# Moving g's high parts, the weights, x and g's low parts to other residues modulo 512 bytes in SBUF

## The chip, the cores and the metric

The kernel runs on one core of a Trainium2 chip. The metric is the time of one execution in microseconds (us) of device time. Before the change three runs gave a median of 848.11 us.

## The reference

Eight batches of eight heads (sequence 576, head dimension 64) go through a linear attention: q is normalised over the head dimension, k over the sequence, and q meets the 64x64 product of k and v. The result, seen as 4608 rows of 512, goes through a two-layer network with relu squared between the layers.

```
q_s = exp(q - max(q, axis=-1));  q_s = q_s / (sum(q_s, axis=-1) + 1e-09)
k_s = exp(k - max(k, axis=2));   k_s = k_s / (sum(k_s, axis=2) + 1e-09)
kv  = einsum('bhsd,bhse->bhde', k_s, v)
x   = einsum('bhsd,bhde->bhse', q_s, kv)  -> (4608, 512)
r   = maximum(x @ w_in, 0)                # (4608, 2048)
g   = s * (r * r) + b
out = g @ w_out                           # (4608, 512), all float32
```

## The kernel before

The precision of float32 is reached with three matmuls where one would do. Each operand is split into a high part of type float32r, which TensorE takes in one pass, and a low part (the remainder, float32r too). A product is high by high, high by low and low by high. So x is held as xh and xl, each weight as w[:, 0] and w[:, 1], and g as gh and gl.

The 4608 rows are taken in blocks of 512 tokens, the last block being the 64 left-over rows of all eight batches. For each block and each of 16 chunks of 128 of the 2048 hidden columns there is one step t. It has two halves:

- `h_parts` (L1328): 12 matmuls of 512 columns make h for the chunk. The stationary operand is a 128x128 piece of a weight tile `w`, the moving operand is a 512-wide row of xh or xl.
- `o_parts` (L1400): 12 matmuls of 512 columns add the chunk to four accumulators. The stationary operand is a 128x128 piece of gh or gl, the moving operand is a 512-wide row of a weight tile `w`. For each quarter j the order is (gh, w high), (gh, w low), (gl, w high).

Between them ScalarE takes relu out of PSUM into `r` (L1353), ScalarE and VectorE square, scale and shift it, ScalarE rounds it into gh, and VectorE writes gl = r - gh (L1363, L1372, L1379 and others). `gh` and `gl` have two buffers each in the pool `gpool`, used in turn, and `r` has one. Four of the blocks go through a scheme with seven products in place of eight (`product`, L1123; "q" and "qa" in the rows). The last block's second layer is `final` (L1314; "last" in the rows). Its gh and gl lie in weight tiles, not in `gpool`.

Attention of later batches runs beside this on the other engines, a few of its matmuls (L352 kv, L489, L499, L791) between the steps. Every matmul has its load of the stationary operand, an instruction of its own (LDWEIGHTS, engine PEld in the rows), which runs while the matmul before it is still under way.

The order of all instructions on an engine is fixed by hand: generators yield pieces, `Order.run` plays them against planned times, and the list `FIRST` fixes the first ones. `tc.manual_schedule` keeps that order. The tile pools then decide only the addresses, each pool's tiles one after the other in the order of the pools, and the waits that follow from the buffers. Nearly all of SBUF is in use.

Addresses below are bytes within a partition. Most large tiles are a multiple of 512 bytes long, so one shift at the head moves all of them alike. Before the change a tile of 128 bytes with no use but its size (`tiny.tile([P, 32], F32, name="before", ...)`) stands in the first pool, and all the large tiles start at 0 modulo 512. Slices of 128 columns are 512 bytes and rows of 512 columns 2048 bytes, so every stationary piece and every moving row of the 512-column matmuls starts at 0 modulo 512 too.

Of the kernel before, what the change touches and what calls it, by code (L numbers as in the profile page):

```python
# [8 lines left out]
F32 = mybir.dt.float32  # L9
F32R = mybir.dt.float32r  # L10
# [15 lines left out]
def attention_moe(ctx: ExitStack, tc: tile.TileContext, q, k, v, w_in, w_out, s, b, out):  # L26
# [51 lines left out]
    def pool(name, bufs=1):  # L78
        return ctx.enter_context(tc.tile_pool(name=name, bufs=bufs))

    tiny, const, work = pool("tiny", 4), pool("const"), pool("work")
    gpool, xpool, wpool = pool("gpool", 2), pool("xpool", 2), pool("wpool", NFC + 1)
    wide_, small, ends, qpool, sums_q = pool("wide"), pool("small", 4), pool("ends"), pool("qpool", 2), pool("sums", 2)
    dram = ctx.enter_context(tc.tile_pool(name="dram", bufs=1, space=bass.MemoryType.DRAM))
    ps = ctx.enter_context(tc.tile_pool(name="ps", bufs=1, space=bass.MemoryType.PSUM))


    tiny.tile([P, 32], F32, name="before", tag="before", bufs=1)
    ident = const.tile([P, P], F32, name="ident")
    make_identity(nc, ident)  # L90

    kvboth = const.tile([P, 2, 2, 2, D], F32, name="kvf")
    kvfs = [kvboth[:, i] for i in range(2)]
    nc.gpsimd.memset(kvboth, 0.0)
    sb = ends.tile([P, 24], F32, name="sb")
    s_col, b_col = sb[:, 0:1], sb[:, 1:2]
    half = [slice(h * D, (h + 1) * D) for h in range(2)]

# [280 lines left out]
    def k_stream(u):  # L379
        pr, i = divmod(u, 2)  # L380
        due, (tag, bufs) = DUE_K[u], wide(u)
        yield Op("PE", 1.1, due, needs=[f"k{u} there"], take=["big", "ke"])
        kt = by_head(tiles[pr][0])[:, 2 * i:2 * i + 2]
        kT = ps.tile([P, 2, 512], F32, name=f"kT_{u}", tag="big").rearrange("p a b -> p (a b)")
        for n in range(NT):
            for h in range(2):
                nc.tensor.matmul(kT[half[h], n * P:(n + 1) * P], kt[:, h, n], ident, start=True, stop=True)
        yield Op("DVE", 0.67, due)
        km = tiny.tile([P, 1], F32, name=f"km_{u}", tag="km")
        nc.vector.tensor_reduce(out=km, in_=kT[:, 0:S], axis=AX.X, op=ALU.max, negate=True)  # L390
        yield Op("ACT", 0.78, due, free=["big"], gives=[f"z{u}"])
        if pr not in zs:
            zs[pr] = tiny.tile([P, 2], F32, name=f"z_{pr}", tag="z")
        ke = early[:, 0:S]
        nc.scalar.activation(ke, kT[:, 0:S], AF.Exp, bias=km, accum_out=zs[pr][:, i:i + 1])

        yield Op("PE", 0.55, due, take=[tag], free=["ke"])
        kn = ps.tile([P, 2, 512], F32, name=f"kn_{u}", tag=tag, bufs=bufs).rearrange("p a b -> p (a b)")
        for n in range(NQ):
            nc.tensor.transpose(kn[:, n * P:(n + 1) * P], ke[:, n * P:(n + 1) * P], ident)  # L400
        nc.tensor.transpose(kn[0:LEFT, TB:TB + P], ke[:, TB:S], ident)
        yield Op(KN_ON[u], 0.7 if KN_ON[u] == "ACT" else 0.82, due, free=[tag], gives=[f"k{u}"])
        copy = copier(KN_ON[u])
        copy(kt[:, :, 0:NQ], kn[:, 0:TB].rearrange("p (n h d) -> p h n d", n=NQ, h=2))
        copy(kt[0:LEFT, :, NQ], kn[0:LEFT, TB:TB + P].rearrange("p (h d) -> p h d", h=2))
# [29 lines left out]
    def kv_second(pr):  # L435
        due = DUE_V[pr]
        yield Op("PE", 1.4, due, needs=[f"k{u}" for u in (2 * pr, 2 * pr + 1)] + [f"v{pr} there"], take=["sm"], gives=[f"kv{pr}"])
        kv = ps.tile([P, 512], F32, name=f"kv_{pr}", tag="sm", bufs=1)[:, 0:2 * (D + 1)].rearrange("p (u e) -> p u e", u=2)
        heads(kv, by_head(tiles[pr][0]).rearrange("p (u h) n d -> p u h n d", u=2), v_of(tiles[pr][2]))
        yield Op("DVE", 0.33, due)  # L440
        z = tiny.tile([P, 2], F32, name=f"z_{pr}", tag="z")
        scales(z, kv[:, :, D])
        yield Op("ACT", 1.03, due, free=["sm"], gives=[f"kvf{pr}"])
        blocks(pr, kv[:, :, 0:D], z)
# [14 lines left out]
    def q_stream(u):  # L459
        pr, i = divmod(u, 2)  # L460
        bb, hp = divmod(u, NP)
        due, (tag, bufs) = DUE_Q[u], wide(u)

        before = [f"kv{NP // 2 - 1}"] + [f"qe{u}" for u in range(NP - 2, NP)]
        yield Op("DVE", 0.76, due, needs=[f"q{pr} {i} there" if pr == 0 else f"q{pr} there"])
        qt = by_head(tiles[pr][1])[:, 2 * i:2 * i + 2]
        qm = small.tile([P, 2, NT], F32, name=f"qm_{u}", tag="qm")
        nc.vector.tensor_reduce(out=qm, in_=qt, axis=AX.X, op=ALU.max)
        yield Op("DVE", 0.73, due)
        nc.vector.tensor_tensor(out=qt, in0=qt, in1=bc(qm, [P, 2, NT, D]), op=ALU.subtract)  # L470
        yield Op("ACT", 0.74, due, take=["qe"], gives=[f"qe{u}"])
        qn = qpool.tile([P, 2 * NT * (D + 1)], F32, name=f"qe_{u}", tag="qe", bufs=2)
        qe = qn.rearrange("p (n h e) -> p n h e", h=2, e=D + 1)

        nc.gpsimd.memset(qe[:, :, :, D:D + 1], 1e-9)
        nc.scalar.activation(qe[:, :, :, 0:D].rearrange("p n h d -> p h n d"), qt, AF.Exp)
        yield Op("DVE", 0.74, due)
        qs = sums_q.tile([P, NT, 2], F32, name=f"qs_{u}", tag="qs", bufs=2)
        nc.vector.tensor_reduce(out=qs, in_=qe, axis=AX.X, op=ALU.add)
        yield Op("DVE", 0.18, due)  # L480
        nc.vector.reciprocal(qs, qs)
        yield Op("DVE", 0.73, due)

        qn = qn[:, 0:NT * P].rearrange("p (n h d) -> p n h d", h=2, d=D)
        nc.vector.tensor_tensor(out=qn, in0=qe[:, :, :, 0:D], in1=bc(qs, [P, NT, 2, D]), op=ALU.mult)
        yield Op("PE", 0.6, due, take=[tag, "qf"], free=["qe"])
        qT = ps.tile([P, 2, 512], F32, name=f"qT_{u}", tag=tag, bufs=bufs).rearrange("p a b -> p (a b)")
        for n in range(NT):
            nc.tensor.transpose(qT[:, n * P:(n + 1) * P], qn[:, n].rearrange("p h d -> p (h d)"), ident)  # L489
        yield Op(QF_ON[u], 0.55 if QF_ON[u] == "ACT" else 0.66, due, free=[tag])  # L490
        qf = early[:, NT * P:NT * P + S]
        copier(QF_ON[u])(qf, qT[:, 0:S])
        yield Op("PE", 1.0, due, needs=[f"kvf{pr}"] + before * (bb > 0), take=[tag], free=["qf"])

        HB = TB // 2
        xh, xl = x_tile(bb)
        xp = ps.tile([P, 2, 512], F32, name=f"xp_{u}", tag=tag, bufs=bufs)
        for a, src in enumerate((slice(0, HB), slice(HB, S))):
            nc.tensor.matmul(  # L499
                xp[:, a, 0:src.stop - src.start], kvfs[pr % 2][:, i].rearrange("p h d -> p (h d)"), qf[:, src],  # L500
                start=True, stop=True
            )
        yield Op("ACT", 0.82, due, needs=[f"out{u - 4}"] if u >= 4 else (), gives=[f"left{u} there"])
        xh, xl = [t[:, hp, :].rearrange("p (a c) -> p a c", a=2) for t in (xh, xl)]
        nc.scalar.copy(xh, xp[:, :, 0:HB])
        nc.scalar.copy(left_of(u), xp[:, 1, HB:HB + LEFT])
        yield Op("DVE", 0.6, due, free=[tag], gives=[f"x{u}"])
        nc.vector.tensor_tensor(out=xl, in0=xp[:, :, 0:HB], in1=xh.bitcast(F32), op=ALU.subtract)


    def k_tiles(pr):
        m2 = bits[:, 2 * P:6 * P].rearrange("p (h n d) -> p h n d", h=4, n=2)
        m1 = bits[:, 6 * P:8 * P].rearrange("p (h d) -> p h d", h=4)
        return m2, m1, tiny.tile([P, 2], F32, name=f"km_{pr}", tag="km")

    def k_max_2(kt, m2):
        nc.vector.tensor_tensor(out=m2, in0=kt[:, :, 0:2], in1=kt[:, :, 2:4], op=ALU.max)
# [106 lines left out]
    def q_late(u):  # L624
# [9 lines left out]
        if on_act:  # L634
            yield Op("ACT", 0.6, due, take=["qe"])
            qe = qpool.tile([P, 2, 2, NT, SQ], F32, name=f"qe_{u}", tag="qe", bufs=2)
            qs = sums_q.tile([P, 2, NT], F32, name=f"qs_{u}", tag="qs", bufs=2)
            for h in range(2):
                for n in range(NT):
                    if (h, n) in ((0, 2), (0, 4), (1, 1), (1, 3)):  # L640
# [6 lines left out]
        else:  # L647
# [4 lines left out]
            qe = qpool.tile([P, 2, 2, NT, SQ], F32, name=f"qe_{u}", tag="qe", bufs=2)  # L652
            nc.scalar.activation(qe, qt_, AF.Exp)
            yield Op("DVE", 0.76, due)
            qs = sums_q.tile([P, 2, 2, NT], F32, name=f"qs_{u}", tag="qs", bufs=2)
            nc.vector.tensor_reduce(out=qs, in_=qe, axis=AX.X, op=ALU.add)
            yield Op("DVE", 0.5, due)
            nc.vector.scalar_tensor_tensor(
# [50 lines left out]
    def kv_late(pr):  # L709
# [10 lines left out]
        kv = kv[:, 0:2 * (D + 1)].rearrange("p (u e) -> p u e", u=2)  # L720
        heads(kv, by_head(kt).rearrange("p (u h) n d -> p u h n d", u=2), v_of(vt))
        yield Op("DVE", 0.5, due)
        z = tiny.tile([P, 2], F32, name=f"z_{pr}", tag="z")
        nc.vector.tensor_scalar(z, kv[:, :, D], 1e-9, None, op0=ALU.add)
        nc.vector.reciprocal(z, z)

# [465 lines left out]
    def quadrant(p, n):  # L1192
# [59 lines left out]
            w = win(t % NFC)  # L1252
            gh, gl = w[:, 0], w[:, 1]
        else:
            gh = gpool.tile([P, TB], F32R, name=f"gh_{t}", tag="gh")
            gl = gpool.tile([P, TB], F32R, name=f"gl_{t}", tag="gl")
        G[t] = (gh, gl)
        if on:
# [10 lines left out]
    def second_block(n):  # L1269
# [12 lines left out]
        yield Op("ACT", 0.52, due, needs=[there], take=["g"])  # L1282
        if n < 2:
            r = kept(f % 2)
        gh = gpool.tile([P, TB], F32R, name=f"gh_{t}", tag="gh")
        gl = gpool.tile([P, TB], F32R, name=f"gl_{t}", tag="gl")
        G[t] = (gh, gl)
        nc.scalar.copy(gh, r)
# [28 lines left out]
    G = {}  # L1317
    acc = {}

    def h_parts(t):  # L1320

        blk, f = divmod(t, NFC)
# [9 lines left out]

    def g_tiles(t):
        r = gpool.tile([P, TB], F32, name=f"r_{t}", tag="r", bufs=1)
        gh = gpool.tile([P, TB], F32R, name=f"gh_{t}", tag="gh")
        gl = gpool.tile([P, TB], F32R, name=f"gl_{t}", tag="gl")
        G[t] = (gh, gl)
        return r, gh, gl
# [257 lines left out]
```

## Time and profile before

| | |
|---|---|
| median of 3 runs (lowest, highest) | 848.11 us (848.05, 848.28) |
| the profiled execution's own time | 849.44 us |
| its span, first to last instruction | 847.6 us |
| mean granted TensorE clock in the span | 0.997 of 2.4 GHz |
| TensorE matmul busy | 835.3 us, 99% of the span |
| VectorE, ScalarE, GpSimd busy | 574.5, 517.3, 177.7 us |

The profiled execution is 1.84 us longer than its span and 1.33 us longer than the median run. In the rows PE is the matmul side of TensorE, PEld its loads of the stationary operand, DVE VectorE, ACT ScalarE, POOL GpSimd. Matmuls overlap in the trace: one begins while the drain of the one before it is still shown. So the cost of one in a stream is the distance from its start to the next one's start, called the step below, and not the mean duration of a row.

### The profile page before, as it was taken

The numbers are of one execution on the slowest core, as the hardware profiler recorded it, in microseconds if no ns is written. First come the engines' busy times: TensorE is split into PE (matmuls) and PEld (weight loads), VectorE is DVE, ScalarE is ACT, GpSimd is POOL, SyncE is SP. The second block draws the span as 40 slices with busy tenths as digits, with TensorE's granted clock in tenths as the row PEclk, the third lists the DMA queues.
The fourth block names the chain that finished last, engine by engine and source line by source line (L and its number), as shares of the span: only waits on it lengthen the run. The fifth ranks groups of instructions, "written<-read, shape, count | busy, mean of one in ns | idle before, by whom it ended". The sixth has DMA issues, their size and how long they took to land.

```text
span 847.6 us, 12317 instructions
## 1 busy us (share of the span) xinstructions
PE 835.3 (99%) x4344; PEld 689.3 (81%) x4344; DVE 574.5 (68%) x898; ACT 517.3 (61%) x907; POOL 177.7 (21%) x199
## 2 busy tenths in 40 slices
PE   7999999999999999999999999999999999999997
PEld 6788888888888888888888887878888888888886
DVE  5999875696887897887857896874454644556300
ACT  4999975566675646755667667676663367455400
POOL 1000002354122453231402431421101021111000
PEclk9999999999999999999999999999999999999999
DMA  8978039945465667456582636875289320100100
GB/s 262 334 256 285 2 86 318 345 123 144 149 183 129 173 157 206 143 129 165 172 227 67 169 109 212 228 229 161 87 306 377 87 100 26 50 25 1 50 26 25
DMA packets 130401, 134.03 MB, mean 158 GB/s; under 512 B 63012, under 2 KB 107044, under 8 KB 130212
## 3 DMA queue, kind: packets, MB, share of 16 engines
q1 hardware_dynamic: 129184, 132.13, 51.2%
q10 hardware_dynamic: 1156, 1.11, 0.4%
q8 instruction: 34, 0.56, 0.3%
q14 instruction: 27, 0.22, 0.1%
HBM read 89.13 MB, written 35.70 MB: 147 GB/s over the span
## 4 chain that ended last, share of the span: by engine, by line
PE 90%; DVE 4%; ACT 2%; DMA 2%; issue 1%; SPq 1%; ACTq 0%; DVEq 0%
PE acc L1400 39%; PE h L1328 25%; PE q L1123 14%; PE last L1314 5%; PE qa L1123 2%; PE kv L352 2%; DMA st<-in_moe_w_in_dram 1%; DMA area<-in_q_dram 1%; PE xp L499 1%; PE xp L791 1%; DVE y L759 1%; PE xq L791 1%; DVE w L894 0%; ACT low L247 0%; DVE zone L1229 0%
## 5 line engine op out<-in xcount | busy, mean ns | idle before, releaser
L1400 PE MATMUL acc<-w,gh 128*128 128x512 f32 x992 | 307.0, 391 | 0.0
L1328 PE MATMUL h<-x,w 128*128 128x512 f32 x960 | 235.7, 391 | 0.5 <-ACT r L1353 0.5
L1400 PEld LDWEIGHTS acc<-w,gh 128*128 128x128 f32 x992 | 184.6, 188 | 38.1
L1328 PEld LDWEIGHTS h<-x,w 128*128 128x128 f32 x960 | 178.8, 188 | 37.9 <-ACT r L1353 0.7
L1400 PE MATMUL acc<-w,gl 128*128 128x512 f32 x496 | 193.4, 390 | 0.0
L1400 PEld LDWEIGHTS acc<-w,gl 128*128 128x128 f32 x496 | 93.1, 188 | 19.9 <-DVE gl L1372 0.3
L1353 ACT ACTIVATE r<-h 128x512 f32<-128x512 f32 x80 | 47.7, 597 | 73.5 <-PE h L1328 72.7
L1123 PE MATMUL q<-w,w 128*128 128x512 f32 x188 | 47.3, 390 | 0.0
L649 POOL TENSOR_TENSOR area<-area,qm 128x640 f32<-128x640 f32 x22 | 29.8, 1362 | 81.8 <-DVE qm L632 49.3
L667 POOL TENSOR_TENSOR qe<-qe,qr 128x640 f32<-128x640 f32 x24 | 31.7, 1319 | 54.7 <-DMA mb<-maxima 23.6
L1123 PEld LDWEIGHTS q<-w,w 128*128 128x128 f32 x188 | 35.1, 188 | 7.6 <-ACT r L1216 0.3
L1314 PE MATMUL last<-w 128*128 128x512 f32 x168 | 38.7, 389 | 0.0
L1375 DVE SCALAR_TENSOR_TENSOR r<-r,sb 128x512 f32<-128x512 f32 x36 | 29.9, 832 | 12.7 <-ACT r L1353 12.4
L1265 DVE SCALAR_TENSOR_TENSOR gl<-r,sb,gh 128x512 fp32r<-128x512 f32 x24 | 20.2, 843 | 26.5 <-ACT gh L1263 26.5
L1363 DVE TENSOR_TENSOR gl<-r,gh 128x512 fp32r<-128x512 f32 x24 | 19.3, 804 | 27.4 <-ACT gh L1361 27.3
L1314 PEld LDWEIGHTS last<-w 128*128 128x128 f32 x168 | 31.5, 188 | 6.6
L1377 ACT ACTIVATE gh<-r,sb 128x512 fp32r<-128x512 f32 x36 | 26.0, 723 | 12.1 <-DVE r L1375 11.7
L1379 DVE SCALAR_TENSOR_TENSOR gl<-r,sb,gh 128x512 fp32r<-128x512 f32 x36 | 29.1, 809 | 5.4 <-ACT gh L1377 5.1
L998 POOL TENSOR_TENSOR sum<-sum 128x256 f32<-128x256 f32 x32 | 31.4, 980 | 1.6
L1428 ACT COPY last<-last 128x512 f32<-128x512 f32 x3 | 1.8, 586 | 42.0 <-PE last L1314 42.0
L740 POOL TENSOR_TENSOR spare<-kvf,spare 128x256 fp32r<-128x256 f32 x12 | 10.8, 902 | 72.3 <-issue 55.6
L1249 DVE SCALAR_TENSOR_TENSOR r<-r,sb 128x512 f32<-128x512 f32 x24 | 18.0, 752 | 11.6 <-ACT r L1220 5.6
(245 smaller groups left out, 1451.7 us busy)
## 6 DMA issues: line engine op xcount, KB each, us to landing
w<-w_kept SPq DMA_DIRECT2D x28, 512.0 KB, 5.5
st<-in_moe_w_in_dram SPq DMA_DIRECT2D x16, 512.0 KB, 7.6
st<-in_moe_w_out_dram SPq DMA_DIRECT2D x16, 512.0 KB, 8.0
w_kept<-w SPq DMA_DIRECT2D x16, 512.0 KB, 8.3
out_dram<-o SPq DMA_DIRECT2D x16, 512.0 KB, 5.0
turned<-area SPq DMA_DIRECT2D x24, 320.0 KB, 2.4
qT<-turned SPq DMA_DIRECT2D x48, 160.0 KB, 3.2
area<-in_k_dram SPq DMA_DIRECT2D x14, 512.0 KB, 4.3
```

Of the source, the lines that this page charges most:

```text
L649: nc.gpsimd.tensor_tensor(out=qt, in0=qt, in1=bc(qm, [P, 2, NT, D]), op=ALU.subtract)
L667: nc.gpsimd.tensor_tensor(out=qe_, in0=qe_, in1=qr, op=ALU.mult)
L998: nc.gpsimd.tensor_tensor(out=o, in0=x, in1=y, op=op)
L1123: nc.tensor.matmul(BANK[where], w(l)[:, c * P:(c + 1) * P], xs[m][:, c], start=k in (0, 1, 3) and n == 0, stop=n == 5, skip_group_check=True)
L1265: nc.vector.scalar_tensor_tensor(out=gl, in0=r, scalar=b_col, in1=gh.bitcast(F32), op0=ALU.add, op1=ALU.subtract)
L1314: nc.tensor.matmul(t_, g[:, js], w_, start=(f == 0 and i == 0), stop=(f == NFC - 1 and i == 2))
L1328: nc.tensor.matmul(hp_, w[:, j, c, :], x[:, c, :], start=(c == 0 and i == 0), stop=(c == NP - 1 and i == 2))
L1353: nc.scalar.activation(r, hp_, AF.Relu)
L1375: nc.vector.scalar_tensor_tensor(out=r, in0=r, scalar=s_col, in1=r, op0=ALU.mult, op1=ALU.mult)
L1377: nc.scalar.activation(gh, r, AF.Identity, bias=b_col)
L1379: nc.vector.scalar_tensor_tensor(out=gl, in0=r, scalar=b_col, in1=gh.bitcast(F32), op0=ALU.add, op1=ALU.subtract)
L1400: nc.tensor.matmul(acc[blk, j // 2][:, j % 2], g[:, js], w_, start=(f == 0 and i == 0), stop=(f == NFC - 1 and i == 2))
```

## The change

It moves tiles in SBUF. `high_tile` gives each gh buffer 128 bytes more than it uses, so gh's first buffer stays at 0 modulo 512, the second comes to 128, and gl and all that lies behind it come to 256. To make room, the 128-byte tile at the head goes, `sb` and the small sums `qs` move into the first pool, `z` moves out of it into a pool at the end, and four pools of small tiles have fewer buffers (km 4 to 3, z 4 to 3, qm 4 to 3).

Start addresses modulo 512, as the two programs have them:

| tile | before | after |
|---|---|---|
| ident, kvf, misc, early, qhl, tmp tiles (low, o, mb, y, sum), r | 0 | 0 |
| gh, first and second buffer | 0, 0 | 0, 128 |
| gl, both buffers | 0, 0 | 256, 256 |
| x, raw1, t34 | 0 | 256 |
| weights (st, w, spare, zone, w_back, set1) | 0 | 256 |
| area, area_late, last | 0 | 256 |
| qe, qT, first and second buffer | 448, 0 | 32, 96 |

On every engine the same instructions stand in the same order with the same waits as before. Only the addresses differ, and the row length of gh's tile in the access patterns.

```
-    tiny, const, work = pool("tiny", 4), pool("const"), pool("work")
+    tiny, few, const, work = pool("tiny", 2), pool("few", 3), pool("const"), pool("work")
     gpool, xpool, wpool = pool("gpool", 2), pool("xpool", 2), pool("wpool", NFC + 1)
-    wide_, small, ends, qpool, sums_q = pool("wide"), pool("small", 4), pool("ends"), pool("qpool", 2), pool("sums", 2)
+    wide_, small, qpool, sums_q, zpool = pool("wide"), pool("small", 3), pool("qpool", 2), pool("sums", 2), pool("zpool", 3)
+    ends = tiny
...
-    tiny.tile([P, 32], F32, name="before", tag="before", bufs=1)
...
-    sb = ends.tile([P, 24], F32, name="sb")
+    sb = ends.tile([P, 24], F32, name="sb", tag="sb", bufs=1)
...
-        km = tiny.tile([P, 1], F32, name=f"km_{u}", tag="km")
+        km = few.tile([P, 1], F32, name=f"km_{u}", tag="km")
...
-            zs[pr] = tiny.tile([P, 2], F32, name=f"z_{pr}", tag="z")
+            zs[pr] = zpool.tile([P, 2], F32, name=f"z_{pr}", tag="z")
...
-        qs = sums_q.tile([P, NT, 2], F32, name=f"qs_{u}", tag="qs", bufs=2)
+        qs = tiny.tile([P, NT, 2], F32, name=f"qs_{u}", tag="qs", bufs=2)
...
+    def high_tile(t):
+        return gpool.tile([P, TB + 32], F32R, name=f"gh_{t}", tag="gh")[:, 0:TB]
+
...
         r = gpool.tile([P, TB], F32, name=f"r_{t}", tag="r", bufs=1)
-        gh = gpool.tile([P, TB], F32R, name=f"gh_{t}", tag="gh")
+        gh = high_tile(t)
         gl = gpool.tile([P, TB], F32R, name=f"gl_{t}", tag="gl")
```

The other changed lines repeat these for further tiles of km, z, qs and gh.

## Rows read from the trace of the kernel before

**Rows 1.** The page, part 1: busy us, share of the span, instructions
```profile
PE 835.3 (99%) x4344; PEld 689.3 (81%) x4344; DVE 574.5 (68%) x898; ACT 517.3 (61%) x907; POOL 177.7 (21%) x199
```

**Rows 2.** Stretches, core 0: length, busy us of each engine, granted clock, DMA, GB/s
```profile
0.00:21.00 21.00, 15.76 (x161) 14.11 (x161) 12.39 (x21) 9.77 (x21) 3.50 (x20) 0.92 0.84 261
21.00:42.00 21.00, 19.40 (x154) 15.62 (x155) 20.66 (x35) 19.43 (x39) 0.30 (x4) 1.00 1.05 333
42.00:106.00 64.00, 64.00 (x326) 52.73 (x324) 58.48 (x77) 59.91 (x80) 1.35 (x7) 1.00 0.53 183
...
742.00:847.00 105.00, 101.33 (x448) 83.56 (x446) 32.36 (x44) 32.50 (x54) 4.38 (x4) 0.99 0.08 26
```

**Rows 3.** What PE waited for, us in total, times, longest: the three longest
```profile
PE kn L400 <- ACT early L395: 3.1, 2, 2.7
PE unused L1538 <- POOL ident masks.py:199: 2.5, 1, 2.5
PE q L1123 <- ACT zone L1216: 0.5, 2, 0.4
```

**Rows 4.** The page, part 5: matmul groups with 512 columns, and one of loads
```profile
L1400 PE MATMUL acc<-w,gh 128*128 128x512 f32 x992 | 307.0, 391 | 0.0
L1328 PE MATMUL h<-x,w 128*128 128x512 f32 x960 | 235.7, 391 | 0.5 <-ACT r L1353 0.5
L1400 PEld LDWEIGHTS acc<-w,gh 128*128 128x128 f32 x992 | 184.6, 188 | 38.1
L1400 PE MATMUL acc<-w,gl 128*128 128x512 f32 x496 | 193.4, 390 | 0.0
L1123 PE MATMUL q<-w,w 128*128 128x512 f32 x188 | 47.3, 390 | 0.0
L1314 PE MATMUL last<-w 128*128 128x512 f32 x168 | 38.7, 389 | 0.0
```

**Rows 5.** The chain that ended last: start us, length us, what, instructions
```profile
2.05 6.36 DMA area<-in_q_dram
...
14.00 6.79 DMA st<-in_moe_w_in_dram
...
27.08 0.97 PE xp L499 x4
...
51.95 2.72 PE h L1328 x12
...
70.27 2.77 PE h L1328 x12
...
639.33 38.08 PE acc L1400 x168
...
800.49 42.85 PE last L1314 x189
```

**Rows 6.** Timeline of PEld and of PE at 400 us: start us, length us
```profile
400.74 2.68 PEld L1328 LDWEIGHTS h<-x,w 128*128 128x128 f32 x12
...
400.96 2.88 PE L1328 MATMUL h<-x,w 128*128 128x512 f32 x12
```

**Rows 7.** Timeline of PE at 175 us: L791 with 320 and 256 columns
```profile
174.90 0.31 PE L791 MATMUL xp<-qhl,spare 128*128 128x320 f32 x1
175.04 0.28 PE L791 MATMUL xq<-qhl,spare 128*128 128x256 f32 x1
175.16 0.31 PE L791 MATMUL xp<-qhl,spare 128*128 128x320 f32 x1
175.31 0.28 PE L791 MATMUL xq<-qhl,spare 128*128 128x256 f32 x1
175.43 0.62 PE L1400 MATMUL acc<-w,gh 128*128 128x512 f32 x2
```

**Rows 8.** Timeline of PE at 68 and 101 us: one 512-column matmul ahead of L489
```profile
68.41 0.39 PE L1400 MATMUL acc<-w,gl 128*128 128x512 f32 x1
68.64 0.71 PE L489 MATMUL qT<-ident,qe 128*128 128x128 f32 x5
...
101.55 0.40 PE L1400 MATMUL acc<-w,gl 128*128 128x512 f32 x1
101.79 0.71 PE L489 MATMUL qT<-ident,qe 128*128 128x128 f32 x5
```

**Rows 9.** Lines L1363 and L1218: duration ns min/median/max, first and last start
```profile
L1363 DVE TENSOR_TENSOR gl<-r,gh x24: 681/693/1666, 52.6 to 482.9; 128x512 fp32r<-128x512 f32 x24
...
L1218 DVE TENSOR_TENSOR misc<-q,misc x16: 691/691/693, 684.9 to 793.7; 128x512 f32<-128x512 f32 x16
```

**Rows 10.** DMA issues, KB each, median us from issue to landing
```profile
area<-in_k_dram SPq DMA_DIRECT2D x2, 256.0 KB, 5.0
...
raw<-in_k_dram SPq DMA_DIRECT2D x2, 256.0 KB, 5.3
```

More of the change, by code (lines that the diff above doesn't have):

```diff
@@ L440, in kv_second @@
         yield Op("DVE", 0.33, due)
-        z = tiny.tile([P, 2], F32, name=f"z_{pr}", tag="z")
+        z = zpool.tile([P, 2], F32, name=f"z_{pr}", tag="z")
         scales(z, kv[:, :, D])
@@ L513, in k_tiles @@
         m1 = bits[:, 6 * P:8 * P].rearrange("p (h d) -> p h d", h=4)
-        return m2, m1, tiny.tile([P, 2], F32, name=f"km_{pr}", tag="km")
+        return m2, m1, few.tile([P, 2], F32, name=f"km_{pr}", tag="km")
     def k_max_2(kt, m2):
@@ L636, in q_late @@
             qe = qpool.tile([P, 2, 2, NT, SQ], F32, name=f"qe_{u}", tag="qe", bufs=2)
-            qs = sums_q.tile([P, 2, NT], F32, name=f"qs_{u}", tag="qs", bufs=2)
+            qs = tiny.tile([P, 2, NT], F32, name=f"qs_{u}", tag="qs", bufs=2)
             for h in range(2):
@@ L654, in q_late @@
             yield Op("DVE", 0.76, due)
-            qs = sums_q.tile([P, 2, 2, NT], F32, name=f"qs_{u}", tag="qs", bufs=2)
+            qs = tiny.tile([P, 2, 2, NT], F32, name=f"qs_{u}", tag="qs", bufs=2)
             nc.vector.tensor_reduce(out=qs, in_=qe, axis=AX.X, op=ALU.add)
@@ L722, in kv_late @@
         yield Op("DVE", 0.5, due)
-        z = tiny.tile([P, 2], F32, name=f"z_{pr}", tag="z")
+        z = zpool.tile([P, 2], F32, name=f"z_{pr}", tag="z")
         nc.vector.tensor_scalar(z, kv[:, :, D], 1e-9, None, op0=ALU.add)
@@ L1284, in second_block @@
             r = kept(f % 2)
-        gh = gpool.tile([P, TB], F32R, name=f"gh_{t}", tag="gh")
+        gh = high_tile(t)
         gl = gpool.tile([P, TB], F32R, name=f"gl_{t}", tag="gl")
@@ L1334, in g_tiles @@
         r = gpool.tile([P, TB], F32, name=f"r_{t}", tag="r", bufs=1)
-        gh = gpool.tile([P, TB], F32R, name=f"gh_{t}", tag="gh")
+        gh = high_tile(t)
         gl = gpool.tile([P, TB], F32R, name=f"gl_{t}", tag="gl")
```

## The prediction

> **What bounds the kernel now.** I read the page's busy times first, then the stretches, the waits of PE, the groups of matmuls, and last the chain and the timeline for the step of one matmul. PE is busy for 835.3 of 847.6 us [rows 1]. What it lacks lies at the two ends: 5.24 and 1.60 us in the first 42 us, and 3.67 us in the stretch from 742 us on, which holds the last copy and store [rows 2]. From 42 to 106 us it is busy for all of 64.00 us [rows 2]. Its own waits are small: the two longest are 3.1 and 2.5 us and both belong to the start, the third is 0.5 us in all [rows 3]. So VectorE, ScalarE, GpSimd and the DMAs set nothing between 42 us and the end. The time there is the number of matmuls times their step.
>
> That step is very even. A run of 168 second-layer matmuls takes 38.08 us, 226.7 ns each, and a run of 189 at the end takes 42.85 us, 226.7 ns each [rows 5]. Twelve of the first layer take 2.72 us, again 226.7 ns [rows 5]. The five largest groups hold 992 + 960 + 496 + 188 + 168 = 2,804 such matmuls [rows 4], or 636 of the 847.6 us.
>
> At the granted clock of 1.00 [rows 2] 512 columns need 512 / 2.4 = 213.3 ns. So each step holds 13.3 ns that are not columns. The load of the next stationary operand begins with the matmul before it: the twelve loads of one h begin at 400.74 us, one step before its matmuls at 400.96 [rows 6], and each lasts 188 ns [rows 4]. Two streams are thus read from SBUF side by side in every step, the moving row of this matmul and the stationary piece of the next, and before the change both start at 0 modulo 512. Whether the 13.3 ns come from where these two lie is the whole question.
>
> **The change part by part.** Instructions, order and waits are the same, so nothing is added or removed, and only the durations can move.
>
> *First, the stationary pieces of gh.* These are 992 loads, and 32 more against the weights that were fetched back, 1,024 in all (only the 992 are shown [rows 4]). Before, each lies at the same residue as the moving row over which it is loaded. After, it lies 256 bytes from it in the steps of gh's first buffer and 128 bytes in those of the second, about 512 loads each. Loads of gl against w, of w against x, and those of the last block keep a distance of 0, since both sides move by 256. No row shows a steady 512-column stream with such a distance, so I bound the price by the nearest rows.
>
> Bound above: a stream that has just been broken by smaller matmuls is slower, twelve matmuls taking 2.77 instead of 2.72 us, 4.2 ns more each [rows 5]. So the step is not a constant of the matmul; it can settle elsewhere. At 4.2 ns the 1,024 steps cost 4.3 us. A single pair of rows points the same way. The matmul ahead of L489's loads takes 0.24 us where the buffer of qe lies at 448 modulo 512 (101.55 to 101.79), and 0.23 where it lies at 0 (68.41 to 68.64) [rows 8]. That is at most 10 ns in one event, and would be 10.2 us over 1,024.
>
> Bound below: four matmuls in plain float32, two of 256 and two of 320 columns, take 0.97 us [rows 5]. At half the rate, one column in two cycles, their 1,152 columns need 0.96 us, so there a load leaves only about 2.5 ns per matmul. If a distance made the loads of gh as cheap, each step would lose 10.8 ns, 11.1 us over 1,024.
>
> The value I take is zero. L791 is the only full-rate stream with a distance. Its moving operand starts at 0 for 320 columns and at 256 for 256 columns, in runs of 128 bytes that jump by 640, while its stationary operand stays at 0. Four of them take 175.43 - 174.90 = 0.53 us [rows 7] for 1,152 columns, which need 0.48. That leaves 12.5 ns per matmul, give or take 2.5 ns for the rounding, beside 13.3 in the streams with distance 0. So the extra seems to come with each load, whatever the distance and the number of columns. This row is nearest, because it runs at full rate, and it speaks for no change.
>
> *Second, VectorE's and ScalarE's work on r, gh and gl.* gl = r - gh reads two tiles at residue 0 and writes a third there, with a median of 693 ns; the sum that reads one of its operands from PSUM takes 691 [rows 9]. Equal residues cost VectorE nothing that could be given back. Even a gain would be covered, since PE waits for neither engine after the start [rows 3]. Zero.
>
> *Third, what DMAs write.* The q, k, v and weight tiles now start at 256. This matters only at the start, where two DMAs stand on the chain, 6.36 and 6.79 us [rows 5]. No row has a landing at 256. Two places of one kind, 256 KB each, differ by 0.3 us at equal residues [rows 10], so I bound it at 0.3 us either way for each of the two, 0.6 us in all, and take zero. Later the qT tiles leave 448 and 0 for 32 and 96; PE does not wait there.
>
> *Fourth, fewer buffers of km, z and qm.* A missing buffer could make an engine wait for an old reader. The two programs have the same waits, so this is zero with no range.
>
> The sum is the profiled execution's 849.44 us plus 0, within -11.1 and +10.2 us for the first term and 0.6 us for the third. The median run is 1.33 us below the profiled one. **The forecast is 848.1 us**, by itself 847.0 to 849.2.
>
> [...]
>
> **The rivals.**
>
> *Faster: the 13.3 ns are a meeting of the two reads.* Both streams begin at the same residue within nanoseconds. If that is the worst case, a distance of 128 or 256 spares part of it. For it: the half-rate rows lose only 2.5 ns [rows 5]. Against it: L791 with a distance pays as much [rows 7]. If one of the two gh buffers gains all of it, 512 x 10.8 = 5.5 us give 842.6; both give 837.0.
>
> *Slower: the new distance is the worse one.* Place: the two steps in three of the second layer in which a gh piece is loaded over a moving row of w. Today's 226.7 ns would be the good phase, into which a stream settles after 2.77 us per twelve [rows 5], and a shifted load would hold it out of it. For it: the 0.24 beside 0.23 us [rows 8]. It decides the sign from 1.7 ns per step on, which is 0.2% of the time over 1,024. At 4.2 ns it gives 852.4, at 10 ns 858.3.
>
> *The change does not do what it says.* Residues might not matter to any engine at all, and then all that is left is the start. This is the forecast too, 847.5 to 848.7.
>
> **How the numbers follow.** About 0.2%, 1.7 us, is what a measurement of this kernel can tell from no change. No change beyond that has 0.46: L791 and the evenness of the step speak for it, but no row holds a long stream with a distance. Faster has 0.31, since the matmul step is the only thing left to gain from and 13.3 ns stand in it unexplained. Slower has 0.23, resting on the transient and on one event. The likeliest single case is no change, though the two others hold 0.54 together. The range takes in the middle of the faster rival and the nearer end of the slower one: 841.0 to 853.0. It leaves out the cases in which both gh buffers gain nearly all, or in which the loss is over 5 ns per step, about 0.1 each.
>
> **What would show it.** In the profile after, twelve matmuls of L1400 in a steady stream should still take 2.72 us, as twelve of L1328, whose distance is 0 before and after. If L1400 differs and L1328 does not, the distance decides, and the difference between even and odd steps tells 256 from 128. If both differ, the residue itself decides, not the distance. The last block, L1314, keeps distance 0 and should keep 226.7 ns. gl of L1363 should keep 693 ns. A longer start would show as idle time of PE before 42 us, now 6.84 us. The prediction is wrong if PE's busy time moves by more than 1.7 us, or if PE begins to wait for VectorE, ScalarE or a DMA in mid-kernel.

## The result and the profile after

The changed kernel is slower: a median of 854.75 us (853.83 to 856.11) against 848.11 (848.05 to 848.28), a ratio of 1.0079 with a 95% interval of 1.0062 to 1.0097. Its profiled execution took 854.19 us with a span of 852.4 us, 4.8 us more than the span before. Runs of the kernel before that were taken with the experiments have medians of 848.55 to 849.43 us and lie between 847.66 and 852.03, so the spread of the changed kernel's runs is not its own, and its loss is between 5.3 and 6.6 us, by the runs it is measured from.

The busy times of the page after, which answer to [rows 1]:

```profile
PE 841.4 (99%) x4344; PEld 690.0 (81%) x4344; DVE 572.3 (67%) x898; ACT 517.5 (61%) x907; POOL 177.7 (21%) x199
```

PE is busy 6.1 us longer with the same 4,344 matmuls. The busy times of the other engines moved by 2.2 us at most. The stretches at the two ends, as in [rows 2], the first from 0 to 42 us in two pieces:

```profile
0.00:21.00 21.00, 16.88 (x171) 14.96 (x172) 13.66 (x24) 11.17 (x25) 3.57 (x20) 1.00 0.84 266
21.00:42.00 21.00, 19.42 (x152) 15.47 (x151) 20.66 (x33) 19.49 (x37) 0.23 (x2) 1.00 1.06 340
42.00:106.00 64.00, 64.00 (x324) 52.46 (x323) 57.72 (x76) 59.50 (x80) 1.26 (x7) 1.00 0.53 179
```

PE lacks 5.70 us in the first 42 us, where it lacked 6.84, so the start has not become longer. The granted clock of its first 21 us is 1.00 here and was 0.92: the kernel before was granted 0.66 of the clock from 12 to 15 us, 0.77 from 15 to 18, and 0.50 from 13 to 16, where this one was granted 1.00. That is not the change. Among the experiments below, which run the same instructions in the same order, these 21 us come out either way: 1.00 in ctl0, s256 and x128, 0.92 in s128, gl128 and g0_256. From 42 to 106 us PE is busy throughout, but gets through 324 matmuls in place of 326.

What PE waited for is again the start and half-microseconds (compare [rows 3]):

```profile
PE unused L1541 <- POOL ident masks.py:199: 2.5, 1, 2.5
PE kn L400 <- ACT early L395: 1.9, 3, 1.4
PE h L1331 <- ACT r L1356: 0.5, 1, 0.5
```

So the step has grown. Lines 1400 and 1328 of before are 1403 and 1331 now. The chain, start and length in us, in one stretch of mid-kernel and in the two long runs of [rows 5]:

```profile
158.75 2.73 PE h L1331 x12
161.48 2.81 PE acc L1403 x12
164.28 2.72 PE h L1331 x12
167.00 2.72 PE acc L1403 x12
...
184.54 2.81 PE acc L1403 x12
187.34 2.72 PE h L1331 x12
```

```profile
641.80 38.73 PE acc L1403 x168
...
805.25 42.85 PE last L1314 x189
```

The twelve matmuls of L1403 alternate: 2.81 us, then 2.72, then 2.81, one step t after the other, as gh's two buffers do. The twelve of the first layer keep 2.72 to 2.73. The 168 of the second layer, half of them with the second buffer, took 38.08 us and take 38.73. The 189 of the last block, which read no gh from `gpool`, keep 42.85 to the hundredth. So, as the prediction put it, L1403 differs and L1331 does not, and the two gh buffers differ from each other.

### The profile page after: what moved, and what is told of

Same layout as the page of the kernel before. It is cut to its first block, busy times and chain, and to the rows that moved or that the text cites. A ratio compares the mean times of both kernels' runs of the same rounds, so it can differ in the third digit from the quotient of the medians.

```text
span 852.4 us, 12317 instructions
## 1 busy us (share of the span) xinstructions
PE 841.4 (99%) x4344; PEld 690.0 (81%) x4344; DVE 572.3 (67%) x898; ACT 517.5 (61%) x907; POOL 177.7 (21%) x199
## 4 chain that ended last, share of the span: by engine, by line
PE 89%; DVE 5%; DMA 3%; SPq 2%; issue 1%; ACT 1%; ACTq 0%; DVEq 0%
PE acc L1403 39%; PE h L1331 25%; PE q L1123 13%; PE last L1314 5%; PE qa L1123 2%; PE kv L352 2%; DMA raw<-in_v_dram 1%; DMA st<-in_moe_w_out_dram 1%; DMA area<-in_q_dram 1%; PE xp L791 1%; PE xp L499 1%; PE xq L791 1%; DVE y L759 1%; SPq L338 0%; SPq L332 0%
## 5 line engine op out<-in xcount | busy, mean ns | idle before, releaser
L1403 PE MATMUL acc<-w,gh 128*128 128x512 f32 x992 | 311.1, 395 | 0.0
L1331 PE MATMUL h<-x,w 128*128 128x512 f32 x960 | 236.3, 392 | 0.5 <-ACT r L1356 0.5
L1403 PEld LDWEIGHTS acc<-w,gh 128*128 128x128 f32 x992 | 185.2, 188 | 40.6
L1331 PEld LDWEIGHTS h<-x,w 128*128 128x128 f32 x960 | 179.1, 188 | 38.4 <-ACT r L1356 0.7
L1403 PE MATMUL acc<-w,gl 128*128 128x512 f32 x496 | 194.9, 393 | 0.0
L1403 PEld LDWEIGHTS acc<-w,gl 128*128 128x128 f32 x496 | 93.2, 188 | 21.2
```

The source lines that it names most:

```text
L1331: nc.tensor.matmul(hp_, w[:, j, c, :], x[:, c, :], start=(c == 0 and i == 0), stop=(c == NP - 1 and i == 2))
L1403: nc.tensor.matmul(acc[blk, j // 2][:, j % 2], g[:, js], w_, start=(f == 0 and i == 0), stop=(f == NFC - 1 and i == 2))
```

## The experiments

All kernels below have the instructions, the order and the waits of the kernel before; they differ in addresses alone. Each group of runs was compared with its own runs of the kernel before, whose medians were 849.17, 848.55 and 849.43 us in the three groups, so the ratios count and not the times.

Theory **distance**: the step depends on how far the stationary piece being loaded lies from the moving row that is read at the same time, modulo 512 or 256, and 128 is bad. Rivals: **residue** (a stationary piece off a multiple of 256 is bad by itself), **small tiles** (the smaller and moved pools, or qe and qT), and **g's other users** (ScalarE writing gh and VectorE reading it meet PE).

### The pads alone undone: ctl0

```
-        return gpool.tile([P, TB + 32], F32R, name=f"gh_{t}", tag="gh")[:, 0:TB]
+        return gpool.tile([P, TB], F32R, name=f"gh_{t}", tag="gh")[:, 0:TB]
```

> The changed kernel without the 128 bytes behind each gh buffer: the pools of small tiles stand as after the change, all large tiles start at 0 modulo 512 again. If the loss comes from where gh stands (distance or residue), this is the time of before, 848.1 us, and twelve matmuls of L1400 take 2.72 us in every step. If it comes from the smaller or moved pools of small tiles, or from qe and qT, it stays near 854.7.

849.32 us, ratio 1.0003 (0.9990 to 1.0015), and the 168 matmuls take what they took before:

```profile
638.25 38.08 PE acc L1403 x168
```

All the rest of the change, pools and fewer buffers, is in this kernel and costs nothing that can be measured. The small tiles are out.

### gh at 128, 384 and 256, all else at 0: s128, s384, s256

From here on the kernels start from ctl0, except g0_256, which starts from the changed kernel. gh gets a pool of its own behind `area`, which ends 96 bytes past a multiple of 512; a pad of 32, 288 or 160 bytes sets its residue.

```
-    wide_, small, qpool, ... = pool("wide"), pool("small", 3), ...
+    wide_, hpool, small, qpool, ... = pool("wide"), pool("hpool", 2), pool("small", 3), ...
...
+    hpool.tile([P, 8], F32, name="pad", tag="pad", bufs=1)
...
-        return gpool.tile([P, TB], F32R, name=f"gh_{t}", tag="gh")[:, 0:TB]
+        return hpool.tile([P, TB], F32R, name=f"gh_{t}", tag="gh")
```

> All large tiles at 0 modulo 512, both gh buffers at 128 (gh stands in a pool of its own behind area). Theory distance (what counts is how far the stationary piece lies from the moving row modulo 512, and 128 is bad either way round): every step of L1400 with gh is slow, so twice the loss of the change, about 861. Theory sign (only a stationary piece 128 below its moving row, that is 384 above, is bad): 848.1 here. Theory residue (a stationary piece that does not start at a multiple of 256 is bad, wherever the moving row is): about 861 too.

> All large tiles at 0 modulo 512, both gh buffers at 384. This is the distance of the slow buffer in the changed kernel (its gh at 128, its w at 256), now in both buffers and with other residues. Theory distance, and theory sign: about 861, steps of L1400 at 233 ns in place of 227. Theory residue: about 861. If the loss needs the very residues 128 and 256, 848.1.

> All large tiles at 0 modulo 512, both gh buffers at 256. Theory distance: as the fast buffer of the changed kernel, so 848.1 us with steps of 227 ns. Theory residue: 848.1 as well. If any distance but 0 costs and the even steps of the changed kernel only hid it, above 852.

s128: 859.39 us, ratio 1.0130 (1.0115 to 1.0145). s384: 861.07 us, ratio 1.0145 (1.0130 to 1.0160). s256: 848.60 us, ratio 0.9999 (0.9989 to 1.0010). The chain of s128, of s384 and of s256 (L1404 is L1400 of before, L1332 is L1328):

```profile
160.44 2.77 PE h L1332 x12
163.21 2.81 PE acc L1404 x12
166.02 2.73 PE h L1332 x12
168.75 2.81 PE acc L1404 x12
...
646.64 39.21 PE acc L1404 x168
```

```profile
645.89 39.21 PE acc L1404 x168
```

```profile
160.46 2.72 PE acc L1404 x12
...
637.64 38.08 PE acc L1404 x168
```

With both buffers at 128 or at 384 twelve of L1404 in an unbroken stream take 2.79 to 2.81 us, in either buffer, and the 168 take 39.21, 233.4 ns each, to the same hundredth of a microsecond for either sign. At 256 they take 38.08, as at 0. So 256 is as good as 0 and 128 is equally bad both ways round. The theory that only one sign hurts falls with s128.

### Distance or residue: all128

```
+    const.tile([P, 32], F32, name="shift")
     ident = const.tile([P, P], F32, name="ident")
```

> One pad of 128 bytes at the head moves every large tile, gh among them, to 128 modulo 512, so that every stationary piece starts at 128 and every distance is 0. Theory distance: 848.1 us, all steps 227 ns. Theory residue (a stationary piece off a multiple of 256 is read badly): all 3,360 steps lose 7 ns, about 871.

849.73 us, ratio 1.0012 (1.0002 to 1.0023): at most 0.2% more, where the residue theory wanted 2.7%. Every large tile starts at 128, and the step is that of 0:

```profile
162.44 2.72 PE acc L1404 x12
165.16 2.72 PE h L1332 x12
...
639.63 38.08 PE acc L1404 x168
```

So the residue of the stationary piece by itself did not matter to the step here, 226.7 ns in the 168 at 128 as at 0. The distance did: 233.4 ns in s128.

### x moved, g left alone: x128

`xpool` goes behind `area` with a pad of 32 bytes. gh, gl and w stay at 0.

```
-    gpool, xpool, wpool = pool("gpool", 2), pool("xpool", 2), pool("wpool", NFC + 1)
+    gpool, wpool = pool("gpool", 2), pool("wpool", NFC + 1)
...
+    xpad.tile([P, 8], F32, name="xpad")
```

> g is left alone: gh, gl and w at 0, and x (with t34, which shares its pool) at 128. No stationary piece of gh or w moves; the moving rows of the first layer do. Theory distance: the 960 steps of h and some 200 of the products now have a distance of 128 and go to 234 ns, about 856 us, while L1400 stays at 227. Theory residue of the stationary piece: 848.1. A theory by which g's own writers and readers (ScalarE writing gh, VectorE reading it) meet the loads: 848.1.

856.14 us, ratio 1.0091 (1.0076 to 1.0106), as the distance theory had it. Now it is the first layer that is slow:

```profile
162.06 2.73 PE acc L1404 x12
164.79 2.79 PE h L1332 x12
167.59 2.73 PE acc L1404 x12
170.32 2.79 PE h L1332 x12
```

gh, gl and all stationary pieces of these matmuls start where they did modulo 512, and g's writers and readers are left alone, so g's other users are out as a cause. A shift of the moving row did what a shift of the stationary piece did, 2.79 us per twelve here and 2.81 in s128, so what counted is how the moving row and the piece loaded beside it lay to each other. Here all loads of the first layer have the same distance, and the stream still does not come back to 2.72. So it is not only the change from one distance to the next that costs.

### One load in three: gl128

```
-            gl = gpool.tile([P, TB], F32R, name=f"gl_{t}", tag="gl")
+            gl = lpool.tile([P, TB], F32R, name=f"gl_{t}", tag="gl")
...
```

The same stands at the other two places where a gl is made. `lpool` lies where `hpool` lay in s128, so gl starts at 128 and gh at 0.

> All large tiles at 0 modulo 512, only gl's two buffers at 128. Now one load in three of L1400, 512 in all, has a distance of 128, where s128 had two in three. Theory per load (a step is slow when the load read beside it, or its own, has the distance): two steps in three, those ahead of and on a gl piece, at 234 ns, the third at 227, so about 855.5. Theory phase (one load with a distance throws the stream out of its settled phase, and it needs some ten matmuls to come back): all three steps of a quarter are slow, some 1,500 steps, and the time is near that of s128, 858 to 860.

854.18 us, ratio 1.0061 (1.0045 to 1.0077).

```profile
159.80 2.72 PE h L1332 x12
162.52 2.77 PE acc L1404 x12
165.30 2.72 PE h L1332 x12
168.02 2.77 PE acc L1404 x12
...
643.20 38.83 PE acc L1404 x168
```

Eight steps at 233 ns and four at 227 are 2.77 us, so the theory per load holds, and the one by which a shifted load costs the ten matmuls behind it falls. The start times of the trace show which steps these are. Where the matmul uses gh and loads gh beside itself, the mean step is 227.5 ns. Where it uses gh and loads gl, 232.4. Where it uses gl and loads gh, 233.8. So here a shifted load costs two steps: the one beside which it runs, and the next, which uses the piece. Why the second is slow too stays open, since the load is then shown as over (188 ns of a 227 ns step). That it is slow because of its own piece is not shown. In s128 the last step of a twelve that is followed by the first layer uses a gl piece at 0 and loads a piece of w at 0, and still takes 231.7 ns (mean of 74, against 227.5 before). In x128 the second and third steps of L1404 behind the first layer neither load nor use a piece that was loaded at a distance, and take 232.4 and 231.1 ns before the fourth is back at 227.2 (means of 69). So a short way back to the even step, of one to three matmuls, fits the runs as well as a cost in the step that uses the piece.

### The second buffer alone put back: g0_256

```
+    pads = []
...
-        return gpool.tile([P, TB + 32], F32R, name=f"gh_{t}", tag="gh")[:, 0:TB]
+        gh = gpool.tile([P, TB], F32R, name=f"gh_{t}", tag="gh")
+        if not pads:
+            pads.append(gpool.tile([P, 64], F32, name="pad", tag="pad", bufs=1))
+        return gh
```

The buffers' pad is one tile of 256 bytes behind the second one. Both gh buffers stand at 0 and gl, x and the weights at 256, as in the changed kernel.

> The changed kernel with one edit undone: both gh buffers at 0 modulo 512, with 256 bytes of pad behind the second, so that gl, x and the weights stay at 256. Only the 128 of the second buffer is gone. Theory distance modulo 256: 848.1 us, steps of L1400 at 227 ns in both buffers. If gl, x and the weights at 256, or qe at 32 and 96, take a part of the loss, it stays above 850.

849.55 us, ratio 1.0001 (0.9988 to 1.0014), and the 168 matmuls (L1408 here) are back:

```profile
639.14 38.08 PE acc L1408 x168
```

So the loss of the change is the 128 of the second gh buffer, as far as these runs can tell a difference (0.14%).

### Other distances: d32_64, d192_224, d16_48

A pad ahead of the two buffers and 32 bytes more per buffer give each run two distances, one per buffer. The places of 16 to 64 are 272 to 320 modulo 512, and count as these distances because 256 counted as 0 in s256. In d16_48 gh starts 16 bytes into its tile:

```
...
+        at = 4
+        return hpool.tile([P, TB + 8], F32R, name=f"gh_{t}", tag="gh")[:, at:at + TB]
```

> All large tiles at 0 modulo 512, gh's first buffer at 288, its second at 320. If only the distance modulo 256 counts, these are distances of 32 and 64, and the two buffers' steps can be told apart in the trace. By the 96 bytes of the changed kernel's set0 (230 ns) and the 128 of its gh (234 ns), a loss that grows with the distance gives 228 and 229 ns, some 850 us. If any of these distances makes the meeting of the two reads rarer than at 0, a step below 226 ns.

> All large tiles at 0 modulo 512, gh's first buffer at 192, its second at 224: 64 and 32 below a multiple of 256. If the sign of the distance does not count, the same steps as with 64 and 32 above it. If it counts, one of the two pairs is slow and the other not, or faster than 226 ns.

> All large tiles at 0 modulo 512, gh's first buffer read from 272, its second from 304: 16 and 48 above a multiple of 256. If what counts is which piece of 32 bytes or more the two reads are in, 16 is as good as 0 and its steps stay at 227 ns, while 48 is slow like 32 and 64 (231 to 235). If any distance off a multiple of 256 spoils the phase, both are slow, about 857 in all. A step below 226 ns in either would be a place that beats both kernels.

One time each, with no interval: 858.17, 856.36 and 853.24 us. The runs of 168 in the three, in that order:

```profile
644.98 38.97 PE acc L1404 x168
```

```profile
643.42 38.87 PE acc L1404 x168
```

```profile
641.90 38.45 PE acc L1407 x168
```

The mean step of a matmul that uses gh and loads gh, from the start times in the traces, breaks over 300 ns left out:

| gh above w, modulo 256 | step, ns | run |
|---|---|---|
| 0 | 227.2, 227.1 | before, s256 |
| 16 | 228.3 | d16_48, first buffer |
| 32 | 231.5 | d32_64, first buffer |
| 48 | 233.6 | d16_48, second buffer |
| 64 | 234.1 | d32_64, second buffer |
| 128 | 234.8, 234.9 | s128, s384 |
| 192 | 230.3 | d192_224, first buffer |
| 224 | 234.8 | d192_224, second buffer |

The loss grows from 0 to 48 bytes and is about the same at 64 and at 128. Between these it is not settled: the one case at 96, some products of the changed kernel (`set0`, a tile in the second qe buffer), shows 229 to 230 ns in 48 steps. Above 128 the loss is uneven, and 64 and 32 below a multiple of 256 (192 and 224) are not 64 and 32 above it. No distance tried gives a step below that of 0, so none of these places beats the kernel before. With one run each, the table rests on the steps within a trace and not on a comparison of times. The expectation that 16 is as good as 0 was nearly met: its median is 227 ns, but a tenth of its steps take 233 or more. The 228 and 229 ns that were expected of 32 and 64 were too low.

## Why the prediction was wrong

**What bounds the kernel** was right. PE stayed 99% busy, nothing began to wait, and the time moved with the step of the matmul alone.

**The first term** failed, and with it the forecast. It was set to zero because L791 had a distance and paid no more [rows 7]. But the distance there was 256 (in its 256-column matmuls, 0 in the others), which s256 and g0_256 show to be as good as 0. The row could speak for the first buffer of gh, not for the second. I let a row at one distance stand for all. The change itself named two distances and the working kept them together; taken apart, the row nearest to 128 was the event with qe at 448, 64 below a multiple of 256 [rows 8], and it pointed the right way. Rounding hid its size: by the start times of the trace before, the step ahead of the loads is 236 ns there and 230 where qe lies at 0. In the long streams, 64 below costs 3 ns (192 in the table) and 64 above 7 ns.

**The price** was mis-sized as well. The 4.2 ns of the broken stream [rows 5] stood for a load with a distance; the runs show 6 to 8 ns in each step of the second buffer. In the changed kernel these are 235.1 ns (uses gh, loads gh), 234.5 (uses gh, loads gl) and 233.2 (uses gl, loads gh) against 227.2. The 504 shifted loads slow all three steps of a quarter, 756 in place of 504, because the step behind a shifted load pays too. 249 x 7.9 + 252 x 7.3 + 161 x 6.0 ns, for the steps that lie within L1403, make 4.8 of the 6.1 us by which PE's busy time grew. The rest lies at the seams to other lines, in the products that load from a buffer of qe at 96 (about 230 ns each), and in 0.3 ns more per step of the first layer.

**The slower rival** came nearest: a shifted load keeps the stream from its 226.7 ns. It had the loss in two steps of three and in both buffers, where it is three of three in one buffer. Its 852.4 us lay below the result, and the range, which ended a little above it at 853.0, missed 854.75. Its good phase, into which a stream settles and out of which a shifted load holds it, is neither shown nor ruled out. gl128 is against a long way back, the third step being fast again. But one stretch is for it. At about 156 us forty small attention matmuls (L352 in the kernel before) break the stream. The twelves behind them are, first in the kernel before and then in s128:

```profile
156.47 2.95 PE acc L1400 x12
159.42 2.72 PE h L1328 x12
...
157.46 2.98 PE acc L1404 x12
160.44 2.77 PE h L1332 x12
```

With distances of 0 the stream has settled within the first twelve. In s128, where these twelve have shifted loads, the twelve of the first layer behind them, at distance 0, are still unsettled (224 to 236 ns for eight steps).

**The faster rival** falls. None of the distances tried gave a mean step below the 226.7 ns of distance 0, so nothing of the 13.3 ns was to be had there. What these are stays open. Their size, and the 2.5 ns of the half-rate rows, came from 2.4 columns per ns and half of that. The trace before shows near to it: steps of 118 ns with 256 columns and 148 with 320 (L791), and 226.7 with 512. That is 0.42 ns for each column more from 256 to 512 and 0.41 from 320, by which 512 columns take an estimated 209 to 217 ns and leave 10 to 18. Plain float32, in L489 and L499, has steps of 109, 216 and 269 ns with 128, 256 and 320 columns, 0.83 ns for each column more, which leaves an estimated 2 to 3.

**VectorE and ScalarE** were right: gl keeps its time, with its operands now at three residues (compare [rows 9]).

```profile
L1366 DVE TENSOR_TENSOR gl<-r,gh x24: 683/692/1546, 51.1 to 484.6; 128x512 fp32r<-128x512 f32 x24
```

**The DMAs and the smaller pools** were right too: ctl0 and g0_256 have them and are level with the kernel before. The landings of [rows 10] read 5.1 and 4.7 us in the changed kernel, against 5.0 and 5.3. The second moved by twice the 0.3 us that was allowed, to the better, and the start did not become longer.

## What to carry to other kernels

In a kernel bound, as this one, by streams of float32r matmuls of 512 columns, keep the stationary pieces and the moving rows that are read beside them at the same start modulo 256 bytes; here distances of 0 and 256 bytes gave 226.7 ns a step, and distances of 32 to 128 cost 1 to 3% of every step that they touched. Other types and widths were not run. A pad of 128 bytes behind a double-buffered tile shifts its second buffer and everything after it, so look at the start address of each buffer before and after such a change. When a change sets two values, price each by a row with that value: a row that shows one of them to be harmless says nothing of the other.

## What was not expected of the hardware

The step of a matmul went by how its moving row and the stationary piece loaded beside it lay to each other in SBUF: 226.7 ns per 512-column step at a distance of 0 or 256 bytes, 233.4 at 128 either way in the second layer's order of two shifted loads in three (38.08 and 39.21 us per 168). The cost did not end with the load: one to three matmuls behind it were slow as well, by 4 to 7 ns (233.8 in gl128, 231.7 in s128, 232.4 and 231.1 in x128, against 227), even some that neither load nor use a shifted piece (s128, x128).
